# A decode kernel over two attention layers: one second-pass unit of four rows placed ahead of the next row's kept units

## The chip, the cores and the metric

The kernel runs on one core of one Trainium2 chip. The metric is the device time of one execution in microseconds (us). The time before is the median of five runs, 1151.18 us (1147.98, 1152.47, 1147.93, 1151.68 and 1151.18 us). Where this text says "the profile", it means one further look at the same kernel: an execution of 1147.98 us whose instructions and transfers were recorded.

## What is computed

Eight rows (a batch of 8, one token each, 448 numbers per row) go through attention, a small mixer and MLP, attention again with the same weights and the same cache, and the mixer and MLP again:

```python
def _A_ref(x, k_cache, v_cache, wq, wo):          # Hq = 16 heads, 8 KV heads, Sk = 4096, Dh = 256
    q = (x @ wq) as [B, 16, 1, 256]
    scores = einsum("bhqd,bhkd->bhqk", q, repeat(k_cache, 2)) * 256 ** -0.5
    o = einsum("bhqk,bhkd->bhqd", softmax(scores), repeat(v_cache, 2))
    return o as [B, 1, 4096] @ wo
...
x = x + _A_ref(_layernorm(x), K, V, wq, wo)
x = x + _B_ref(_layernorm(x), w1, w2, w3, w4)     # with one token the shifted parts are zero:
x = x + _A_ref(_layernorm(x), K, V, wq, wo)       # what is left is x1 + gelu(layernorm(x1) @ w3) @ w4
x = x + _B_ref(_layernorm(x), w1, w2, w3, w4)
```

K and V of one row are 8 x 4096 x 256 numbers of two bytes each, 33.6 MB for both. Both attention layers read all of them, and the query of the second reading of a row exists only when the first reading of that row, its output projection, its MLP and its second query projection are done.

## The kernel before, in words

**Units.** A unit is one pass over one pair of KV heads of one row. I write A for the first attention layer's pass and B for the second's: A3.1 is the first pass over row 3, pair 1, and B3.1 the second pass over the same data. A row has four pairs (0 to 3), so there are 64 units. Each is cut into four K chunks and four V chunks of 1 MB. The list `tasks` (L489 to L501) is the order of the units, written out by hand.

**Items.** `items` (L505 to L510) turns the units into single chunks: K chunk j is followed by the V chunk of four K chunks earlier (`LAG` = 4). The main loop (from L664) walks over the items. A K chunk is transposed on DVE in two instructions (L547), and PE multiplies it with the spread query (`scores`, L555). After four K chunks ACT takes the exponentials (L564) and PE transposes them (L577). A V chunk is multiplied on PE (`pv`, L596).

**Slots and loads.** All chunks live in 15 slots of 1 MB (`NC`, L61). `loads` (L516) is the items in order without those that need no load, and `emit_loads` (L522) issues the next load from SP whenever a slot has come free: always in the order of `loads`, so the list of units also sets the order of the transfers.

**Kept chunks.** Eleven chunks of a row stay in their slots from its first pass to its second: all eight of pair 3 and the first three K chunks of pair 2 (`kept`, L63). Pairs 2 and 3 are `keep`, pairs 0 and 1 are `free` in the code. From the last kept load of a row until the second pass of pair 3 gives slots back, only four slots are left to rotate.

**The chain.** Between the two passes of a row stands a sequence of small dependent steps: softmax sums, output projection (L318), norm, MLP (L336, L318), norm, query projection (L274). Its generator `chain` (L441) is added after the last first-pass unit of the row (L735) and is stepped from the main loop by `step` (L645), twice per item, so that its 30 counted steps are spread evenly up to the first item of the row's second pass. `last` (L462) does the smaller work that follows a finished second pass in the same way.

**The order around the change.** For rows 1 to 4 the order before is, with b the row whose second pass runs:

```
B(b).3  B(b).2  |  A(b+1).2  A(b+1).3  |  B(b).0  B(b).1  A(b+2).0  A(b+2).1  |  B(b+1).3  B(b+1).2 ...
```

The chain of row b+1 runs in the units between A(b+1).3 and B(b+1).3. At the two ends of the list (the chains of rows 0, 1, 6 and 7) three units stand there rather than four:

| chain of row | units between its two kept passes |
|---|---|
| 0 | A1.0 A1.1 A2.0 |
| 1 | B0.0 B0.1 A2.1 |
| 2, 3, 4, 5 | B(b).0 B(b).1 A(b+2).0 A(b+2).1, with b = 1 to 4 |
| 6 | B5.0 A7.0 A7.1 |
| 7 | B5.1 B6.0 B6.1 |

Of the kernel before, what the change touches and what calls it, by code (L numbers as in the profile page):

```python
# [17 lines left out]
def kernel(  # L18
# [28 lines left out]
    Bn, Sq, D = A_x.shape  # L47
# [438 lines left out]
    keep = sorted({gp for gp, _, _ in kept})  # L486
    free = [gp for gp in range(GP) if gp not in keep]
    assert Bn > 2 and free == [0, 1] and GP == 4
    tasks = [(0, 0, gp) for gp in free + keep] + [(0, 1, gp) for gp in free]  # L489
# [2 lines left out]
    tasks += [(0, 2, free[0])]  # L492
    for b in range(Bn):
        tasks += [(1, b, gp) for gp in keep[::-1]]
        if b + 1 < Bn:
            tasks += [(0, b + 1, gp) for gp in keep]
        if b == Bn - 2:
            tasks += [(1, Bn - 3, free[-1])]
        tasks += [(1, b, gp) for gp in (free[:-1] if b == Bn - 3 else free)]
        if b + 2 < Bn:  # L500
            tasks += [(0, b + 2, gp) for gp in (free[1:] if b == 0 else free)]  # L501


    nk = 4 * len(tasks)
# [159 lines left out]
    for idx, it in enumerate(items):  # L664
        n, kv, c = it
        ps, b, gp = tasks[n]
# [157 lines left out]
```

## Time and profile before

| what | value |
|---|---|
| median of five runs | 1151.18 us |
| profiled execution | 1147.98 us |
| its span, first to last instruction | 1146.2 us |
| PE (matmul) busy | 702.8 us, 61% |
| DVE busy | 548.1 us, 48% |
| ACT busy | 113.6 us, 10% |
| moved by the DMA engines | 457.52 MB, 399 GB/s over the span |
| chunk loads | 200 of K and 224 of V, 1024 KB each |

The span is the time between the first and the last recorded instruction; 1.8 us of the device time lie around it. A row of "windows" gives, for a stretch of the span in us, its length, the busy time of each engine with its number of instructions, the granted clock of TensorE as a share of full speed (PEclk), the busy share of the DMA engines, and the rate in GB/s at which they moved data. A chunk is 1.0486 MB.

### The profile page before, as it was taken

Reading aid. Unit: us, or ns where it says so; the run is one execution under the profiler, and the core shown is the slowest. Engines: PE = TensorE matmul, PEld = TensorE weight load, DVE = VectorE, ACT = ScalarE, POOL = GpSimd, SP = SyncE. Lnnn points to the kernel's source line nnn. Section 1 sums busy time; section 2 is a strip of 40 time slices with the busy share of each in tenths; the row PEclk is TensorE's granted clock in tenths of the full one; section 3 lists DMA queues with packets and bytes.
Section 4 is the critical chain, followed back from the end, with each engine's and each line's share of the span. In section 5 each row is a group of like instructions: output and inputs, shape, how many; then the busy total and the mean of one; then the engine's idle time right before and its main releaser. Section 6 shows DMA issues by size and latency. Waiting matters only on the chain.

```text
span 1146.2 us, 36707 instructions
## 1 busy us (share of the span) xinstructions
PE 702.8 (61%) x17177; PEld 512.9 (45%) x17177; DVE 548.1 (48%) x904; ACT 113.6 (10%) x234; POOL 15.6 (1%) x25
## 2 busy tenths in 40 slices
PE   3144677457755667556764667646765477547786
PEld 2023455345533445344542455425543365426566
DVE  5145453445444544445355553446434553546352
ACT  0001011100110011101110101010010101010100
POOL 0000000000000000000000000000000000000000
PEclk9999998655755556555565557555575557555655
DMA  9999999999999999999999999999999999999993
GB/s 353 376 420 419 407 367 411 419 416 379 406 420 414 387 388 420 420 404 397 398 419 420 407 406 410 420 421 391 398 420 420 414 384 418 418 419 394 414 420 134
DMA packets 68349, 457.52 MB, mean 399 GB/s; under 512 B 6999, under 2 KB 13030, under 8 KB 13542
## 3 DMA queue, kind: packets, MB, share of 16 engines
q1 hardware_dynamic: 68198, 455.19, 97.9%
q8 instruction: 134, 2.20, 0.8%
q14 instruction: 17, 0.14, 0.0%
HBM read 455.15 MB, written 0.01 MB: 397 GB/s over the span
## 4 chain that ended last, share of the span: by engine, by line
DMA 66%; PE 15%; DVE 12%; SPq 3%; issue 3%; POOL 1%; ACT 0%; POOLq 0%; DVEq 0%; ACTq 0%
DMA slot<-in_A_k_cache_dram 62%; DVE slot L547 10%; PE sc L555 5%; PE o L596 3%; DMA slot<-in_A_v_cache_dram 3%; SPq L148 2%; PE y_ps L318 2%; PE q_ps L274 1%; DMA wq_sb<-in_A_wq_dram 1%; SPq L539 1%; DVE qbd L300 1%; PE o L610 1%; PE o L318 1%; PE misc L381 0%; PE h_ps L336 0%
## 5 line engine op out<-in xcount | busy, mean ns | idle before, releaser
L547 DVE STREAM_TRANSPOSE slot<-slot 128x1024 uint32<-128x1024 uint32 x400 | 472.7, 1222 | 383.2 <-DMA slot<-in_A_k_cache_dram 375.0
L555 PE MATMUL sc<-slot,qbd 128*8 128x128 bf16 x8192 | 280.1, 286 | 344.7 <-DVE slot L547 290.7
L555 PEld LDWEIGHTS <-qbd 128*8 128x8 bf16 x8192 | 193.5, 105 | 429.8 <-issue 296.7
L596 PE MATMUL o<-slot,ptw 128*8 128x256 bf16 x3968 | 242.1, 387 | 54.0 <-DMA slot<-in_A_v_cache_dram 30.7
L564 ACT ACTIVATE p_n<-sc 128x512 bf16<-128x512 f32 x64 | 84.4, 1318 | 780.6 <-PE sc L555 780.6
L596 PEld LDWEIGHTS <-ptw 128*8 128x8 bf16 x3968 | 108.4, 109 | 91.6 <-issue 43.1
L318 PEld LDWEIGHTS <-wo_sb 128*128 128x128 bf16 (+1 forms) x1600 | 64.7, 124 | 16.5 <-issue 15.8
L318 PE MATMUL y_ps<-OT,wo_sb 128*128 128x1 bf16 (+1 forms) x1280 | 55.5, 177 | 3.0 <-issue 3.0
L384 DVE RECIPROCAL rz<-misc 128x8 f32<-128x8 f32 (+1 forms) x33 | 6.3, 192 | 94.8 <-PE misc L381 94.8
L274 PEld LDWEIGHTS <-wq_sb 128*128 128x128 bf16 x1152 | 34.0, 104 | 19.1 <-issue 17.4
L274 PE MATMUL q_ps<-xb,wq_sb 128*128 128x1 bf16 (+1 forms) x1152 | 35.6, 166 | 11.2 <-DMA wq_sb<-in_A_wq_dram 3.6
L584 ACT CAST ptw<-misc 128x128 bf16<-128x128 f32 x64 | 17.5, 273 | 207.5 <-PE misc L577 159.3
L411 PEld LDWEIGHTS misc<-R,o_sb 128*128 128x128 f32 x124 | 26.0, 293 | 11.3 <-issue 11.2
L318 PEld LDWEIGHTS <-w_sb 128*128 128x128 bf16 (+1 forms) x630 | 25.8, 125 | 7.3 <-issue 5.2
L411 PE MATMUL misc<-R,o_sb 128*128 128x8 f32 x124 | 28.9, 343 | 0.0
L232 POOL TENSOR_TENSOR t<-t,nhalf 128x2 f32<-128x2 f32 (+1 forms) x17 | 10.7, 630 | 1071.6 <-DVE t L239 973.0
L318 PE MATMUL y_ps<-HT_t,w_sb 128*128 128x1 bf16 (+1 forms) x560 | 24.2, 177 | 0.5 <-DVE HT_t L359 0.5
L300 DVE TENSOR_SCALAR qbd<-misc,quad 128x64 bf16<-128x64 f32 x64 | 13.8, 278 | 21.0 <-PE misc L294 21.0
L381 PE MATMUL misc<-zm,one 128*128 128x8 f32 (+1 forms) x66 | 17.9, 344 | 6.7 <-ACT ptw L584 6.7
L336 PEld LDWEIGHTS <-w_sb 128*128 128x128 bf16 x560 | 17.1, 104 | 9.5 <-issue 9.1
L336 PE MATMUL h_ps<-xb,w_sb 128*128 128x1 bf16 (+1 forms) x560 | 17.9, 166 | 4.9 <-DVE xb L249 4.6
L381 PEld LDWEIGHTS misc<-zm,one 128*128 128x128 f32 x66 | 15.0, 282 | 11.5 <-ACT ptw L584 8.4
(92 smaller groups left out, 208.0 us busy)
## 6 DMA issues: line engine op xcount, KB each, us to landing
slot<-in_A_v_cache_dram SPq DMA_DIRECT2D x224, 1024.0 KB, 12.3
slot<-in_A_k_cache_dram SPq DMA_DIRECT2D x200, 1024.0 KB, 15.7
wo_sb<-in_A_wo_dram SPq DMA_DIRECT2D x1, 3584.0 KB, 26.6
wq_sb<-in_A_wq_dram SPq DMA_DIRECT2D x3, 1024.0 KB, 6.9
w_sb<-in_B_w_dram SPq DMA_DIRECT2D x1, 1568.0 KB, 12.7
w_sb<-in_B_w_dram SPq DMA_DIRECT2D x3, 448.0 KB, 26.8
wq_sb<-in_A_wq_dram SPq DMA_DIRECT2D x2, 256.0 KB, 9.9
w_sb<-in_B_w_dram SPq DMA_DIRECT2D x2, 112.0 KB, 9.0
```

Source lines behind the costliest of these rows:

```text
L148: nc.sync.dma_start(t[:, fc * cols : (fc + 1) * cols], src[fc * 128 : fc * 128 + 128, :])
L274: nc.tensor.matmul(q_ps[:, j * Hq + h, :], w, xbs(nb)[:, xi, :], start=(fc == 0), stop=(fc == 3),)
L300: nc.vector.tensor_scalar_mul(qbd[:, :, :, a, :], qs.rearrange("p e (f g u h) -> p (e f) u g h", f=2, u=2, h=2)[:, :, u], quad[:, a : a + 1],)
L318: nc.tensor.matmul(r, w[:, i, lo:hi], rhs(i), start=(first and fc == 0 and i == rows[0]), stop=(stop and i == rows[-1]), skip_group_check= ...
L336: nc.tensor.matmul(h_ps[:, c * nb : c * nb + nb], w, xbs(nb)[:, xi, :], start=(fc == 0), stop=(fc == 3),)
L381: nc.tensor.matmul(z_ps, ones, zm[:], start=True, stop=True)
L411: nc.tensor.matmul(ot_ps[:, j], o_sb[:, 128 * j : 128 * j + 128], R[:], start=True, stop=True)
L547: nc.vector.transpose(w, w)
L555: nc.tensor.matmul(sc[32 * k : 32 * k + 8, 128 * x : 128 * x + 128], qbd[:, ep, gp].rearrange("p a h -> p (a h)"), kv[:, k, 2 * half + e2, ...
L564: nc.scalar.activation(p_sb[:].rearrange("p t i x -> p x t i"), sc[:].rearrange("p (x t i) -> p x t i", x=4, t=4), ACT.Exp, scale=scale_ex ...
L584: nc.scalar.copy(ptw[:, :, :, 6:8], pt_ps.rearrange("p t k (a h) -> p a (t k) h", a=4),)
L596: nc.tensor.matmul(o_ps[32 * q : 32 * q + 8, 256 * (g // 4) : 256 * (g // 4) + 256], ptw[:, a, 4 * (y % 4) + y // 4, w : w + 8], v[:, y * ...
```

## The change

For b = 1 to 4 the unit B(b).0 is taken from behind A(b+1).3 and put ahead of A(b+1).2:

```
before: B(b).3 B(b).2        A(b+1).2 A(b+1).3 B(b).0 B(b).1 A(b+2).0 A(b+2).1 B(b+1).3
after:  B(b).3 B(b).2 B(b).0 A(b+1).2 A(b+1).3        B(b).1 A(b+2).0 A(b+2).1 B(b+1).3
```

All other units stand where they stood. `items`, `loads` and the due times of the stepped generators are derived from the list and move with it.

```diff
     for b in range(Bn):
         tasks += [(1, b, gp) for gp in keep[::-1]]
-        if b + 1 < Bn:
+        if b == Bn - 2:
             tasks += [(0, b + 1, gp) for gp in keep]
-        if b == Bn - 2:
-            tasks += [(1, Bn - 3, free[-1])]
-        tasks += [(1, b, gp) for gp in (free[:-1] if b == Bn - 3 else free)]
-        if b + 2 < Bn:
-            tasks += [(0, b + 2, gp) for gp in (free[1:] if b == 0 else free)]
+            tasks += [(1, Bn - 3, free[-1])] + [(1, b, gp) for gp in free]
+        elif b == Bn - 1:
+            tasks += [(1, b, gp) for gp in free]
+        else:
+            early = 0 < b < Bn - 3
+            tasks += [(1, b, free[0])] * early + [(0, b + 1, gp) for gp in keep]
+            tasks += [(1, b, gp) for gp in free[early : 1 if b == Bn - 3 else 2]]
+            if b + 2 < Bn:
+                tasks += [(0, b + 2, gp) for gp in (free[1:] if b == 0 else free)]
```

## The prediction

> **What bounds the kernel now.** I read the page's slices and its chain of work first, then the rate of the transfers stage by stage. On the page:
>
> ```profile
> DMA  9999999999999999999999999999999999999993
> GB/s 353 376 420 419 407 367 411 419 416 379 406 420 414 387 388 420 420 404 397 398 419 420 407 406 410 420 421 391 398 420 420 414 384 418 418 419 394 414 420 134
> ...
> DMA 66%; PE 15%; DVE 12%; SPq 3%; issue 3%; POOL 1%; ACT 0%; POOLq 0%; DVEq 0%; ACTq 0%
> ```
>
> The DMA engines are busy in every slice but the last, and the chain of work runs through loads. But the rate in GB/s is not flat: it stands at 419 to 421 and dips once per row. So the time is bytes over rate, and what can be won is in the dips. 457.52 MB at 420 GB/s would take 1089.3 us; the span is 1146.2 us, so 56.9 us are lost. To place them I cut the span by units, at the ACT instruction (L564) that ends a unit's scores. The stretches from the end of B(b).3 to the end of A(b+1).3 lose nothing; one of them, lengthened by the first unit behind it:
>
> ```profile
> 297.00:361.00 64.00, 36.73 (x884) 25.36 (x887) 31.59 (x33) 6.97 (x14) 0.00 (x0) 0.59 1.01 420
> ```
>
> (The last column is 420, as in six more such stretches.) The stretches from the end of A(b+1).3 to the end of B(b+1).3, where the eleven chunks are kept, the chain of row b+1 runs and B(b+1).3 follows, hold the dips. For the chains of rows 0 to 7, in this order:
>
> ```profile
> core 0: us, PE busy (x) PEld busy (x) DVE busy (x) ACT busy (x) POOL busy (x), PEclk, DMA share, GB/s
> 105.40:181.10 75.70, 52.01 (x1274) 38.58 (x1266) 36.33 (x74) 6.98 (x15) 1.26 (x2) 1.00 0.99 391
> 224.00:297.00 73.00, 47.99 (x1150) 34.67 (x1140) 34.74 (x66) 7.03 (x16) 1.25 (x2) 0.51 1.00 396
> 340.50:434.60 94.10, 57.38 (x1362) 40.98 (x1362) 44.65 (x78) 8.75 (x19) 1.25 (x2) 0.52 1.00 399
> 478.60:571.30 92.70, 57.20 (x1362) 40.73 (x1355) 44.65 (x78) 8.75 (x19) 1.25 (x2) 0.52 0.99 401
> 615.80:706.30 90.50, 57.63 (x1362) 41.36 (x1362) 44.65 (x78) 8.69 (x18) 1.25 (x2) 0.51 1.01 408
> 751.30:843.10 91.80, 57.34 (x1362) 41.27 (x1355) 44.64 (x78) 8.69 (x18) 1.25 (x2) 0.51 1.01 405
> 888.00:959.00 71.00, 46.78 (x1160) 34.22 (x1152) 35.01 (x66) 6.79 (x14) 1.25 (x2) 0.51 1.00 402
> 1003.90:1075.00 71.10, 48.20 (x1150) 35.15 (x1139) 34.59 (x66) 7.07 (x16) 1.25 (x2) 0.51 1.00 407
> ```
>
> Lines 3 to 6 are the four-unit stretches that the change touches; the first two and the last two have three units already. The time lost in a stretch is its length times (1 - rate/420). That gives 5.23 and 4.17 us (rows 0, 1), then **4.71, 4.19, 2.59 and 3.28 us** (four units, sum 14.77, mean 3.69), then 3.04 and 2.20 us. (The remaining 27.5 us lie at the start and the end.)
>
> Where in a stretch? I cut two of them again: at the chain's first DVE step (L373) and at the copy of its last result (L283). A four-unit one, then the stretch of row 6 with three:
>
> ```profile
> 340.50:365.20 24.70, 10.18 (x228) 6.08 (x228) 11.78 (x10) 2.91 (x5) 0.00 (x0) 0.50 1.02 421
> 365.20:419.30 54.10, 36.70 (x854) 27.25 (x854) 29.05 (x58) 4.20 (x10) 1.25 (x2) 0.50 0.98 383
> 419.30:434.60 15.30, 10.50 (x280) 7.66 (x280) 3.83 (x12) 1.63 (x4) 0.00 (x0) 0.59 1.01 420
> ```
>
> ```profile
> 888.00:912.60 24.60, 10.27 (x244) 6.29 (x236) 12.59 (x15) 2.89 (x5) 0.00 (x0) 0.50 1.01 421
> 912.60:946.60 34.00, 27.64 (x660) 21.49 (x663) 18.93 (x45) 2.30 (x6) 1.25 (x2) 0.50 0.99 384
> 946.60:959.00 12.40, 8.86 (x261) 6.44 (x261) 3.50 (x8) 1.59 (x3) 0.00 (x0) 0.57 1.01 416
> ```
>
> The first part runs at 421 although slots are already few: loads issued earlier are still queued. The part with the chain runs at 383 and 384. After the chain the same four slots reach 420 and 416 (in two other stretches 385 and 373, 1.3 and 1.4 us lost, beside steps of `last`). So **the chain's steps cost, more than the four slots alone.** The queue shows why both are needed; loads and SP's longest waits from 361 to 425 us:
>
> ```profile
> slot<-in_A_v_cache_dram SPq DMA_DIRECT2D x14, 1024.0 KB, 8.6
> slot<-in_A_k_cache_dram SPq DMA_DIRECT2D x10, 1024.0 KB, 7.3
> ```
>
> ```profile
> SPq L539 <- DVE slot L547: 20.6, 8, 4.5
> SPq L539 <- PE o L596: 13.0, 10, 2.4
> ```
>
> A load lands there 7.3 to 8.6 us after its issue, about three chunks' worth at 2.50 us each (1.0486 MB at 420 GB/s), where a full queue, from 425 to 478.6 us, shows 19.8. SP sits waiting for transposes and PV products to free a slot. A step of the chain on PE or DVE that delays them by a few us empties a queue this short.
>
> **The change, part by part.** It removes and adds no instruction: the built order has 33962 entries on PE, 633 on DVE and 437 on SP in both versions, and the same bytes. It moves B(b).0 for b = 1 to 4: each time eight loads, eight transposes, 128 score and 64 PV matmuls, and one exponential. The loads pass, on SP's queue, the 16 loads of A(b+1).2 and A(b+1).3.
>
> Where it goes: between B(b).2 and A(b+1).2 all fifteen slots rotate and the rate is 420 (stretch 297 to 361, above). Eight loads more at that rate are 8 x 2.50 = 20.0 us of a full queue: the unit costs its bytes there and nothing else, its DVE work (8 x 1.22 = 9.8 us by the page) and PE work lying beside its transfers. If that cover were gone, the rate of the stretch would show it; its DVE is busy 31.6 of 64 us, so there is room. The kept loads come 20 us later, with the second pass that needs them equally later: nothing is late.
>
> Where it leaves: counted over the order of the items, from the chain's first item to the release of the first kept slot, 24 loads are issued before and 16 after. The unit's 20.0 us of bytes go; so does whatever was lost beside them. **The gain is therefore the loss per stretch with four units minus that with three, times four.** What the chain loses with it, it keeps: its instructions are the same, on 15 items rather than 23, so `step` takes its 30 counted steps at two per item instead of 1.3. What is queued behind a chain step on PE are scores and PV products, and behind those the loads: that is the one wait that grows denser.
>
> The trace of before does not show these rows with three units, so I bound them by the rows that have three. Lowest: 2.20 us (row 7), 4 x (3.69 - 2.20) = 6.0 us faster. Highest: 5.23 us (row 0), 4 x (3.69 - 5.23) = 6.2 us slower. Row 0 is the farthest: nothing but first passes, no `last` beside it, a clock of 1.00 against 0.51. I take the mean of the other three, (4.17 + 3.04 + 2.20)/3 = 3.14 us: 4 x (3.69 - 3.14) = **2.2 us faster**. The parts agree with that size: the chain's own stretch is 52.6 us long and loses 3.33 us on average with four units, 34.9 us and 2.49 with three (by the same cut: rates 383, 396, 402, 393 against 389, 384, 397, without row 0); the denser chain loses more per us (0.071 against 0.063) but for a shorter time.
>
> Sum against the profiled execution: 1147.98 - 2.2 = 1145.8 us. The median of the runs shown is 3.2 us above that execution, the runs lying in two groups near 1148 and 1152. I give the forecast on the median: 1151.18 - 2.2 = **1149.0 us**.
>
> Two places where the rows meet a rule. The trace holds 420 GB/s for 64 us on end and 383 in the worst chain stretch. The Trainium skill, "DMA: Bandwidth & Descriptors", Specifications, gives a limit of about 358 GB/s from HBM for a core; by it 383 would already be at the ceiling, nothing could be won, and the sum would be 0. The measurement decides: the ceiling here is 420. Second, PE is busy 36.7 of 54.1 us in the four-unit chain stretch and 27.6 of 34.0 in the three-unit one, the clock stands at 0.50 in both, and the stretch with 1.00 lost most. The skill's "TensorE: Matmul & The Clock Gate", Part 1, says that sustained work lifts the clock to full; an estimate by it would halve the denser chain's PE time and could take away all 14.77 us. The rows show no such lift at 81% busy, so I add nothing for it.
>
> **The rivals.** (1) *The slots are the cost, the chain only rides on it.* Then the loss goes with the loads issued in the narrow state, 16 instead of 24: 14.77/3 = 4.9 us faster, 1146.3 us. For it: the best three-unit rows, 3.04 and 2.20, are below the four-unit mean by 1.07, near the 1.23 that this asks. Against it: 420 GB/s after the chain with the same four slots.
>
> (2) *The loss belongs to the chain whole, whatever its length.* Rows 0 and 1 together with 6 and 7 have a mean of 3.66 us, the four-unit rows 3.69: 4 x 0.03 = 0.1 us, 1151.1 us. For it: both groups are centred on the same place in the span, and the losses fall with time whatever the number of units. Against it: row 0 carries the mean. This and my forecast are neighbours; both lie within 0.3% of the time before (3.45 us, about what a measurement of this kernel can tell from no change).
>
> (3) *The denser chain costs more than the unit saved: slower.* Two steps per item put two blocks of up to 64 small matmuls between a chunk's scores and the next PV product, in all four stretches. Price: as rows 0 and 1 in the mean, 4.70 us, 4 x 1.01 = 4.0 us slower, 1155.2 us. It decides above a loss of 3.69 + 3.45/4 = 4.55 us per stretch. For it: those two rows. Against it: rows 6 and 7, which have the same fifteen items at the same clock. A chain that is not done when B(b+1).3 starts would add to it; in the rows with three units its last copy is 12 us ahead of the end of B's scores, so it is done in time.
>
> That the change does not do what it says can be left out: the order of the instructions shows the moved unit and nothing else moved.
>
> **How the numbers follow.** Forecast (2.2 us faster, same): 0.36. Rival 1 (faster): 0.32. Rival 2 (same): 0.22. Rival 3 (slower): 0.10. So faster by over 0.3% 0.32, within 0.3% 0.58, slower 0.10. The range reaches down to the low bound of the unknown cost, 1151.18 - 6.0 = 1145.2 us, and up to row 1's loss in all four stretches, 4 x (4.17 - 3.69) = 1.9 us, 1153.1 us; the mean of rows 0 and 1 and row 0 itself are left outside.
>
> **What would show it.** Right: the four stretches from the end of A(b+1).3 to the end of B(b+1).3 are about 71 to 73 us long instead of 90.5 to 94.1, each loses 2.2 to 4.2 us against 420, and the stretch before each is 85 us at 420 instead of 65. Rival 1 shows losses near 2.5 in all four; rival 2 losses as before, 2.6 to 4.7; rival 3 losses over 4.55, with longer SP waits for scores and PV products. Wrong altogether: a rate under 420 in the stretch that takes the unit in, or a chain that ends after the first score of B(b+1).3.

## The result, and the profile after

The changed kernel takes 1151.32 us (median of 27 runs, 1147.31 to 1156.57); the kernel before takes 1150.96 us (median of 48 runs). The ratio is 1.0004, with a 95% interval of 0.9993 to 1.0015: **no difference**. The 2.2 us that were forecast are not there: 0.998 lies outside the interval. The profiled execution took 1153.14 us, its span is 1151.4 us. From its page, the slices and the chain of work:

```profile
DMA  9999999999999999999999999999999999999993
GB/s 354 376 419 420 409 378 401 419 409 367 409 420 420 394 392 420 420 421 380 389 420 420 421 379 396 420 420 404 386 406 420 409 376 416 420 416 371 411 420 147
...
DMA 69%; PE 14%; DVE 10%; SPq 3%; issue 3%; POOL 0%; ACT 0%; POOLq 0%; DVEq 0%; ACTq 0%
```

The bytes are the same and the dips are still there, one per row. The unit went where it was put, and at the price that was forecast. The stretch from the end of B1.3 to the end of A2.3 now holds B1.0; its columns are those of the windows above:

```profile
298.30:361.50 63.20, 35.17 (x884) 24.08 (x887) 31.47 (x33) 7.03 (x14) 0.00 (x0) 0.60 1.01 420
```

It is 63.2 us long at 420 GB/s; without B1.0 the same stretch of before (297.0 to 340.5 us) was 43.5 us: 19.7 us longer, for the 20.0 that were forecast. The eight stretches with a chain, for rows 0 to 7, all with three units now:

```profile
105.20:182.20 77.00, 52.73 (x1274) 39.06 (x1270) 36.43 (x75) 7.01 (x16) 1.26 (x2) 1.00 0.99 392
224.00:298.30 74.30, 48.60 (x1150) 34.88 (x1143) 34.74 (x66) 7.06 (x15) 1.25 (x2) 0.51 0.99 391
361.50:433.90 72.40, 47.80 (x1166) 35.26 (x1159) 35.27 (x70) 7.06 (x16) 1.25 (x2) 0.53 1.00 399
498.50:571.50 73.00, 48.84 (x1166) 35.83 (x1159) 35.40 (x70) 7.09 (x15) 1.25 (x2) 0.51 0.99 392
636.20:709.40 73.20, 48.31 (x1166) 35.70 (x1159) 35.32 (x70) 7.09 (x15) 1.25 (x2) 0.52 1.00 395
773.40:847.10 73.70, 48.94 (x1166) 36.03 (x1155) 35.46 (x70) 7.04 (x16) 1.25 (x2) 0.50 0.99 395
890.80:963.40 72.60, 47.31 (x1160) 34.59 (x1153) 35.02 (x66) 6.83 (x15) 1.25 (x2) 0.51 1.00 397
1007.60:1079.90 72.30, 48.37 (x1150) 35.30 (x1139) 34.69 (x66) 7.04 (x16) 1.25 (x2) 0.51 1.00 395
```

Lines 3 to 6 are some 73 us long instead of 90.5 to 94.1. But by length times (1 - rate/420) they lose 3.62, 4.87, 4.36 and 4.39 us, 17.2 in sum, where the four-unit ones lost 14.77. And the stretches of rows 6 and 7, whose units and order did not change, lose 3.98 and 4.30 us in this execution where they lost 3.04 and 2.20. In e3 below, which has the old order and in these two rows the same steps, they lose 3.62 and 3.76 (399 GB/s over 72.4 us, 398 over 71.7). So a row moves by one to two us between executions without any cause in its own code, and the 0.55 us per stretch that the forecast rested on is smaller than that. The sums 17.2 and 14.77 are those of one execution each, too: the profiled one of before lies 3.0 us below its kernel's median, this one 1.8 us above. The stretch of row 2, cut again at the chain's first and last step:

```profile
361.50:386.80 25.30, 10.18 (x244) 6.36 (x237) 12.53 (x14) 2.90 (x5) 0.00 (x0) 0.50 1.01 420
386.80:421.40 34.60, 28.22 (x662) 21.95 (x665) 19.32 (x49) 2.57 (x7) 1.25 (x2) 0.50 0.99 388
421.40:433.90 12.50, 9.41 (x264) 6.95 (x257) 3.43 (x9) 1.59 (x4) 0.00 (x0) 0.65 0.97 383
```

Queued loads carry the first part, as before. The chain's part lost 2.64 us and the part behind the chain 1.10, at 383 GB/s, where I had read 420 and 416 from two such lines. That part is no clean view of four slots in any of these lines. The kept K chunks of B(b+1).3 are scored in it and give their slots back: in the line of before at 420, PE begins on them at 427.50 us, and SP issues seven loads from 428.58 to 434.49 us, where it had issued four from 420.08 to 426.42. They are not transposed again either, so DVE is busy for only 3.83 of 15.3 us. PE is busy 28.22 of 34.60 us in the middle line, and the granted clock is still 0.50. SP's longest waits (us in total, times, longest) from 386 to 434 us:

```profile
SPq L543 <- PE o L600: 14.2, 9, 2.8
SPq L543 <- DVE slot L551: 10.2, 5, 3.4
```

It waits 14.2 us for PV products in 48 us, where the four-unit stretch of before had 13.0 us in 64: about the same total in a shorter time. For transposes it waits 10.2 us where it had 20.6, so the two waits together, 24.4 us in 48 and 33.6 in 64, are no denser than before.

### The profile page after: what moved, and what is told of

Its sections match the earlier page's. It is cut to its first block, busy times and chain, and to the rows that moved or that the text cites. A ratio compares the mean times of both kernels' runs of the same rounds, so it can differ in the third digit from the quotient of the medians.

```text
span 1151.4 us, 36703 instructions
## 1 busy us (share of the span) xinstructions
PE 703.6 (61%) x17177; PEld 514.1 (45%) x17177; DVE 548.7 (48%) x904; ACT 113.8 (10%) x234; POOL 15.6 (1%) x25
## 4 chain that ended last, share of the span: by engine, by line
DMA 69%; PE 14%; DVE 10%; SPq 3%; issue 3%; POOL 0%; ACT 0%; POOLq 0%; DVEq 0%; ACTq 0%
DMA slot<-in_A_k_cache_dram 64%; DVE slot L551 9%; DMA slot<-in_A_v_cache_dram 4%; PE sc L559 4%; PE y_ps L318 3%; PE o L600 3%; SPq L148 2%; PE q_ps L274 1%; DMA wq_sb<-in_A_wq_dram 1%; SPq L543 1%; PE o L614 1%; PE o L318 1%; PE h_ps L336 0%; DVE qbd L300 0%; POOL t L232 0%
## 5 line engine op out<-in xcount | busy, mean ns | idle before, releaser
L588 ACT CAST ptw<-misc 128x128 bf16<-128x128 f32 x64 | 17.5, 273 | 204.3 <-PE misc L581 155.2
L336 PEld LDWEIGHTS <-w_sb 128*128 128x128 bf16 x560 | 17.5, 104 | 13.9 <-issue 13.5
```

Source lines behind the costliest of these rows:

```text
L336: nc.tensor.matmul(h_ps[:, c * nb : c * nb + nb], w, xbs(nb)[:, xi, :], start=(fc == 0), stop=(fc == 3),)
L588: nc.scalar.copy(ptw[:, :, :, 6:8], pt_ps.rearrange("p t k (a h) -> p a (t k) h", a=4),)
```

## The experiments

Twelve kernels ran, each in five rounds beside the kernel before on the same chip. Ratios are to the kernel before, with the 95% interval.

| run | median us | ratio | interval |
|---|---|---|---|
| old order, no chain (e1) | 1139.31 | 0.9907 | 0.9879 to 0.9934 |
| changed order, no chain (e2) | 1137.93 | 0.9886 | 0.9861 to 0.9911 |
| old order, denser chain (e3) | 1155.28 | 1.0040 | 1.0018 to 1.0062 |
| changed order, one more narrow unit (e4) | 1154.49 | 1.0027 | 1.0009 to 1.0045 |
| changed, step behind PV (e5) | 1156.79 | 1.0045 | 1.0026 to 1.0063 |
| old, step behind PV (e6) | 1152.22 | 1.0006 | 0.9984 to 1.0028 |
| changed, all steps ahead of scores (e7) | 1162.16 | 1.0095 | 1.0064 to 1.0127 |
| changed, 10 kept (e8) | 1149.20 | 0.9980 | 0.9963 to 0.9998 |
| changed, step behind scores (e9) | 1168.34 | 1.0143 | 1.0116 to 1.0170 |
| old, 10 kept (e10) | 1148.55 | 0.9964 | 0.9949 to 0.9978 |
| changed, finer steps (e11) | 1164.25 | 1.0098 | 1.0071 to 1.0125 |
| changed, copy on ACT (e12) | 1152.30 | 1.0026 | 1.0007 to 1.0046 |

After the result I had two theories. Theory 1 was rival 2: the loss belongs to the chain whole. Theory 2: a narrow unit (one that runs with four rotating slots) has a price of its own and was saved, and the chain, which now runs its steps on 15 items rather than 23, took it back.

**The chain left out, in both orders (e1, e2).**

```diff
     def chain(b, st):
-        OT, y_ps = st["OT"], st["y"]
-        yield from half(st["o"], st["z"], 1, OT[:, :, :, 0])
...
         qT = chn.tile([128, NB2], BF16, tag="qT2", bufs=2)
-        yield from project_q(b, 1, qT[:].unsqueeze(2))
+        nc.vector.tensor_copy(qT[:], qT1[:, :, b])
         state[1, b] = {"qT": qT}
+        yield
```

(`first_half` is emptied likewise.)

> Left out: the whole chain between a row's two passes (softmax sums, output projection, MLP, second query projection); the second pass uses a copy of the first query. The order of the units is that of before (four units between the kept passes of rows 2 to 5). Theory 1, the chain's steps cause the loss and the narrow state of four slots costs next to nothing by itself: of the 29.4 us lost in the eight stretches of before, 25 or more go, 1122 to 1127 us. Theory 2, the narrow state costs about 1 us per unit and the denser chain of the change cost about as much, so that the two cancelled: some 10 us stay, 1130 to 1136 us. Under both the first-pass units keep their time.

> Left out: the same chain, in the changed order (three units between the kept passes). Theory 1: the same time as the old order without its chain, within 1.5 us. Theory 2: the four units taken out of the narrow state show now that no chain hides them, 4 us or so faster than the old order without its chain.

By the medians only 12.1 us went in the old order and 13.5 in the changed one. Theory 1 asked for 25 or more; theory 2, with 1130 to 1136 us, had the time too low as well. Over all eight stretches 23.1 us are still lost in e1 and 18.8 in e2, of 29.4 and 35.8 with the chain. The stretches of rows 2 to 5, old order and then changed order, both without a chain:

```profile
338.50:429.60 91.10, 43.42 (x1018) 28.13 (x1011) 40.08 (x45) 8.31 (x17) 0.00 (x0) 0.50 1.00 408
473.70:566.30 92.60, 43.31 (x1018) 28.02 (x1011) 40.18 (x45) 8.23 (x16) 0.00 (x0) 0.51 1.00 401
611.50:702.60 91.10, 43.56 (x1018) 28.13 (x1011) 40.18 (x45) 8.26 (x16) 0.00 (x0) 0.50 1.00 407
746.50:837.60 91.10, 42.16 (x1018) 27.47 (x1009) 40.08 (x45) 8.21 (x16) 0.00 (x0) 0.51 1.00 407
```

```profile
356.20:425.80 69.60, 34.11 (x822) 22.64 (x815) 30.59 (x37) 6.67 (x13) 0.00 (x0) 0.51 1.00 405
490.80:561.30 70.50, 34.65 (x822) 22.91 (x815) 30.59 (x37) 6.65 (x14) 0.00 (x0) 0.51 1.01 410
625.80:697.10 71.30, 34.11 (x822) 22.38 (x813) 30.70 (x37) 6.61 (x13) 0.00 (x0) 0.52 0.99 405
761.10:831.60 70.50, 34.41 (x822) 22.72 (x815) 30.60 (x37) 6.64 (x14) 0.00 (x0) 0.51 0.99 405
```

Without the chain these lines hold the units' own work and the few steps of `last`, and they still lose 2.60, 4.19, 2.82, 2.82 us (12.4) with four units and 2.49, 1.68, 2.55, 2.52 us (9.2) with three. So **the narrow state costs without the chain**. That a unit less of it costs less is likely from this pair and not shown by it: the difference is 3.2 us in these two executions, but row 1, the same in both, differs by 2.5 us (5.12 and 2.60); the ratios of the two runs differ by 0.0021, 2.4 us, with intervals that overlap. Theory 2 had 4. Theory 1 falls, and with it the sentence of the prediction that the chain costs more than the slots.

**The chain's density alone (e3).**

```diff
-    add_gen("chain", b, chain(b, st), idx + 1, first_of[(1, b), 0] - 1, 30)
+    add_gen("chain", b, chain(b, st), idx + 1, idx + 16, 30)
```

> Old order, but the chain of every row is due 15 items after its start, as in the changed order, rather than 23: four units between the kept passes, of which the last has no chain. Theory 1: no difference, 1151 us within 2 us, since the loss goes with the chain's steps and not with their distance. Theory 2: the price of the denser chain without the gain of the shorter narrow state, about 4 us slower than before, 1155 us.

1.0040 times before, 4.6 us slower (2.1 to 7.1), as theory 2 had it. The same units, slots and loads; the chain is done eight items earlier, 17.5 us in the stretch of row 2 (L283 at 401.8 us instead of 419.3). The four stretches:

```profile
341.00:435.70 94.70, 56.30 (x1362) 40.59 (x1351) 45.02 (x78) 8.62 (x18) 1.25 (x2) 0.52 0.99 393
481.00:573.50 92.50, 56.90 (x1362) 41.10 (x1351) 44.94 (x78) 8.64 (x18) 1.26 (x2) 0.51 1.00 397
617.90:711.00 93.10, 56.58 (x1362) 40.90 (x1354) 45.06 (x78) 8.67 (x19) 1.25 (x2) 0.51 1.00 402
755.50:849.10 93.60, 56.25 (x1362) 40.63 (x1351) 44.96 (x78) 8.66 (x19) 1.25 (x2) 0.52 1.00 396
```

They lose 6.09, 5.07, 3.99 and 5.35 us, 20.5 in sum. **About 1.1 us per stretch is the price of two steps per item instead of 1.3.** In units this kernel is also the changed one with its fourth narrow unit given back: from e3 to the changed kernel the ratio falls by 0.0036, 4.1 us, for four narrow units, and the two intervals do not overlap. One thing differs beside the unit. The steps of `last` start behind the chain in e3 (row 2: its first, L373, at 409.4 us) and beside it in the changed kernel (407.5 us, the chain's last at 421.4); what that costs, if anything, is in the 4.1 us and was not measured.

**One narrow unit more, without a chain in it (e4).**

```diff
-        tasks += [(1, b, gp) for gp in keep[::-1]]
+        tasks += [(1, b, free[0])] * (0 < b < Bn - 3) + [(1, b, gp) for gp in keep[::-1]]
...
-            tasks += [(1, b, free[0])] * early + [(0, b + 1, gp) for gp in keep]
+            tasks += [(0, b + 1, gp) for gp in keep]
...
-                elif done == 2:
+                elif done == 2 + (0 < b < Bn - 3) and ps == 1:
```

> Changed order, but for rows 1 to 4 the unit of pair 0 of the second pass comes ahead of the kept units instead of behind them: the chain has the same three units, and one more unit without a chain runs with four slots, in four stretches. Theory 1: the same time as the changed kernel, 1151 us within 2 us. Theory 2: four narrow units at about 1 us each, 1155 us.

1.0027 times before, 0.0023 or 2.6 us above the changed kernel; theory 2 had said 4, theory 1 none. Against before it is slower beyond its interval; against the changed kernel the two intervals touch. Its stretches with the unit, of rows 1 to 4:

```profile
223.30:316.50 93.20, 59.47 (x1360) 42.74 (x1355) 44.85 (x77) 8.96 (x20) 1.26 (x2) 0.50 1.00 404
359.00:453.10 94.10, 57.93 (x1368) 41.66 (x1361) 45.52 (x81) 8.95 (x19) 1.25 (x2) 0.52 1.00 397
497.50:590.20 92.70, 56.68 (x1368) 40.82 (x1357) 45.35 (x81) 8.97 (x19) 1.26 (x2) 0.54 1.00 401
634.40:730.20 95.80, 59.67 (x1376) 43.08 (x1372) 45.17 (x81) 8.99 (x20) 1.26 (x2) 0.50 1.00 400
```

Cut at the ends of the units, the added ones (B1.0 to B4.0, some 20.5 us each) lost 0.4, 0.9, 0.7 and 1.0 us. Whole stretches do not show it: those of rows 1 to 4 lose 17.5 us here and 18.0 in the changed kernel's profile, one execution each. So three ways give the price of a narrow unit by the ratios: 0.6 us (e1 to e2), 0.65 (changed to e4) and 1.0 (e3 to changed). They agree in sign, and the last is clear of its intervals.

**Where the denser chain's price comes from (e5 to e7, e9, e11, e12).** The two-and-two placement of the steps around a K and a V item was shifted. In e5 and e6 the step ahead of the PV products goes behind them:

```diff
-            step(idx)
+            if final:
+                step(idx)
...
         emit_loads()
         step(idx)
+        if kv == 1 and not final:
+            step(idx)
```

> Changed order; of the two chain steps of a V item, the one that stood ahead of the PV products now stands behind them, so that only one step, not two, lies on TensorE between a K chunk's scores and the next PV products. Theory 2a, the denser chain costs through the PV products that wait behind two steps in a row, which frees the V slots late: three to four us come back, 1147.5 us, and SP waits less for PV products. Theory 2b, the chain costs by its total work and its own waits between engines wherever its steps stand: 1151 us within 2 us.

> Old order with the same step moved behind the PV products. Theory 2a: rows 2 to 5 have 1.3 steps per item and seldom two in a row ahead of PV products, so little comes back there, and about one us in each of the four stretches that have three units: 1148 us, slower than or equal to the changed order with the same edit by 1 to 4 us, as the narrow units remain. Theory 2b: 1151 us within 2 us.

Theory 2a falls: the changed kernel got 4.7 us slower by it (1.0045 against 1.0004), and 2b, which had no change, falls too. The old order shows no loss by the same edit (1.0006). So where all eight stretches have two steps per item, the place of a step counts. That it is free with 1.3 is not shown to the microsecond: e6's interval goes up to 3.2 us, and the old order has two steps per item in the four stretches of rows 0, 1, 6 and 7 as well. In e7, which has that edit too, the step behind a K chunk's scores goes ahead of them as well:

```diff
             step(idx)
+            if not final:
+                step(idx)
             scores(sc_t[n % 2], slot, c, st["q"], gp)
```

> Changed order; all four chain steps of a K and a V item stand between the PV products and the next scores, none between scores and PV products. Theory 2a: V slots come free as early as without a chain, but four steps, up to some 4 us of TensorE, can stand ahead of the scores, whose transposes take 2.4 us: 1146 to 1149 us. Theory 2b: 1151 us within 2 us.

Slower again, 1.0095, outside what either theory had. e9 is the mirror image of e5: the step ahead of the scores goes behind them.

```diff
-            step(idx)
+            if final:
+                step(idx)
             scores(sc_t[n % 2], slot, c, st["q"], gp)
...
         emit_loads()
         step(idx)
+        if kv == 0 and not final:
+            step(idx)
```

> Changed order; the mirror image of the step moved behind the PV products: the chain step that stood ahead of a K chunk's scores now stands behind them, so three steps can lie between scores and the next PV products and one between those and the next scores. Theory 3a, what costs is the number of chain steps in a row between two products that free slots, so that the even placement of the changed kernel (two and two) is the best: as bad as the one-and-three placement, 1156 us. Theory 3b, the K chunk's way (transposes, then scores) is the tight one and each step ahead of the scores delays it: three to five us faster than the changed kernel, 1147 us.

1.0143, the slowest of all. Theory 3b falls; of 3a the direction holds (the even placement is the best that was tried), the size does not. Its four stretches lose 7.42, 7.15, 6.09 and 6.51 us:

```profile
366.80:442.80 76.00, 48.17 (x1170) 35.29 (x1164) 35.43 (x70) 7.19 (x16) 1.25 (x2) 0.52 0.98 379
506.70:583.70 77.00, 48.05 (x1174) 35.69 (x1170) 35.59 (x70) 7.15 (x15) 1.25 (x2) 0.52 0.98 381
647.20:722.40 75.20, 48.23 (x1170) 35.45 (x1162) 35.58 (x70) 7.08 (x15) 1.25 (x2) 0.52 0.99 386
785.80:861.80 76.00, 48.63 (x1166) 35.59 (x1157) 35.53 (x70) 7.12 (x15) 1.25 (x2) 0.51 0.98 384
```

Then the same work in smaller portions (e11), with a third `step` in the middle of `scores` and `pv`; the MLP's two projections are cut in the same way:

```diff
-                if h % 8 == 7:
+                if h % (4 if nb == 1 else 8) == (3 if nb == 1 else 7):
                     yield
...
-        yield from add_half(y_ps, OT, 1, 1, False, 2)
+        yield from add_half(y_ps, OT, 1, 1, False, 1)
...
-    add_gen("chain", b, chain(b, st), idx + 1, first_of[(1, b), 0] - 1, 30)
+    add_gen("chain", b, chain(b, st), idx + 1, first_of[(1, b), 0] - 1, 40)
...
         for y in range(16):
+            if y == 8:
+                between()
             q = y % 4
```

> Changed order; the same chain cut into steps of at most 16 matmuls (38 or so rather than 28) and taken at three places per item, the third in the middle of the scores and of the PV products, so that its work lies more evenly between the products. Theory 3a: the stretches lose some 4 to 8 us less, 1144 to 1148 us. If the chain's total work and its waits between engines cost whatever the cut: 1151 us within 2 us.

1.0098: slower, not faster, outside both expectations, so theory 3a in the form "steps in a row" fell too. The length of a step was not changed alone here: the third place lies inside the scores and PV products, and SP's waits for PV products from 386 to 434 us rise from 14.2 to 17.8 us, while those for transposes fall from 10.2 to 4.0. In the kernels with the denser chain DVE waits more for the chain's TensorE results, with the next transposes behind. Over the stretches of rows 2 to 5 I summed from the trace the idle time of DVE ahead of all its instructions but the transposes: 25.5 us before, 60.7 changed, 54.7 in e3, 71.0 in e5, 71.1 in e7, 78.9 in e11, 85.4 in e9, and in e6, which kept its time, 25.5 again. One such wait is that for the chain's last result (L283); idle us and times in the whole execution, before and then changed:

```profile
  PE q_ps L274: 18.5, 5
```

```profile
  PE q_ps L274: 28.6, 9
```

e12 takes just that wait off DVE:

```diff
-        nc.vector.tensor_copy(qT, q_ps[:])
+        if nb == 1:
+            nc.scalar.copy(qT, q_ps[:])
+        else:
+            nc.vector.tensor_copy(qT, q_ps[:])
```

> Changed order; the copy of the chain's last result (L283), ahead of which DVE stands 2.6 us in each of the four stretches with the next K chunk's transposes queued behind it, is done by ACT instead. Theory 4, the denser chain costs because DVE, taking its instructions in order, waits for the chain's TensorE results with transposes behind: of some 60 us of such DVE waits in the four stretches 10.6 go, and the kernel gets 2 to 4 us faster than the changed one, 1148 us. If these waits only accompany the loss: 1151 us within 1.5 us. If ACT's own queue (exponentials and the copies of the transposed weights) suffers by the wait: slower, 1153 us or more.

1.0026: not faster than the changed kernel; its interval takes in both no change and the third outcome, slower by ACT's queue. Of that no sign is in the trace: PE waits for ACT's copies of the transposed weights before its PV products 15.1 us in all, 14.3 in the changed kernel. The wait is gone from DVE (the sum is 51.4 us), the loss is not. So the DVE waits go along with the loss over these kernels, but **that they are its cause is not shown**, and for this one the run speaks against it. With five slots (e8, below) DVE waits 64.7 us by the same sum and the four stretches lose 6.0. What in the denser chain costs stays open; a kernel with the denser chain and several of its DVE waits removed was not run.

**A fifth slot (e8, e10).** Ten kept chunks instead of eleven, in both orders:

```diff
-    kept = [(GP - 1, kv, n) for n in range(4) for kv in range(2)] + [(GP - 2, 0, n) for n in range(3)]
+    kept = [(GP - 1, kv, n) for n in range(4) for kv in range(2)] + [(GP - 2, 0, n) for n in range(2)]
```

> Changed order with ten kept chunks per row instead of eleven, so five slots rotate in the narrow state and eight chunks more are loaded, 20.0 us at 420 GB/s. Theory 2, in both forms, puts the loss on a queue that four slots keep too short: if a fifth slot takes away half of the 36 us lost in the eight stretches of the changed kernel's profile, 1153 us; if it takes two thirds, 1147 us. If the loss were the chain's own time and not the slots, nothing would come back: 1171 us.

> Old order with ten kept chunks. With five slots the stretches of the changed order lost 11 us instead of 36. If both the narrow unit's price and the denser chain's price come from the short queue, both shrink to a third and the two orders stay equal: 1149 us within 2 us. If the chain's density acted by itself, the old order would be the faster one here, 1146 us.

Eight more chunks are loaded, and yet both kernels are faster than before. In the old order, 0.9964, rows 2 to 5:

```profile
339.70:429.20 89.50, 57.07 (x1362) 41.08 (x1355) 44.66 (x78) 8.76 (x19) 1.25 (x2) 0.51 1.01 415
476.80:566.30 89.50, 57.03 (x1362) 40.90 (x1355) 44.64 (x78) 8.79 (x19) 1.25 (x2) 0.51 1.01 413
613.90:703.50 89.60, 56.72 (x1362) 40.76 (x1354) 44.65 (x78) 8.74 (x19) 1.25 (x2) 0.52 1.01 414
750.90:840.00 89.10, 56.54 (x1362) 40.59 (x1355) 44.66 (x78) 8.74 (x19) 1.25 (x2) 0.52 1.00 412
```

In the changed order, 0.9980:

```profile
360.30:432.00 71.70, 48.22 (x1180) 35.76 (x1175) 35.39 (x70) 7.11 (x16) 1.25 (x2) 0.52 1.00 411
497.30:568.80 71.50, 47.97 (x1178) 35.63 (x1174) 35.37 (x70) 7.13 (x16) 1.26 (x2) 0.52 1.01 409
634.30:705.80 71.50, 47.83 (x1180) 35.53 (x1176) 35.36 (x70) 7.12 (x16) 1.25 (x2) 0.52 1.01 413
771.20:843.50 72.30, 47.65 (x1179) 35.50 (x1174) 35.42 (x70) 7.15 (x16) 1.25 (x2) 0.53 1.01 412
```

The old order loses 1.07, 1.49, 1.28 and 1.70 us, 5.5 in place of 14.77, the changed one 6.0 in place of 17.2. All eight stretches together lose some 10.5 us (old) and 11.5 (changed) in place of 29.4 and 35.8. So with a fifth slot about two thirds of the whole loss go, the narrow units' part and the chain's together; the loss needs the short queue. How much of each price is left was not run apart (a denser chain in the old order with ten kept). The two orders differ by 0.0016, within their intervals. e10 is the fastest complete kernel of the study; it beats both orders with eleven.

## Why the prediction was right, and where it was not

- **What bounds the kernel**: right. Bytes over 420 GB/s, and a loss only in the stretches with few slots. In the profiles of all twelve kernels with eleven kept chunks (before and changed among them) the span less the loss of the eight stretches, cut at the ends of the units, lies between 1113.8 and 1117.1 us, while the spans go from 1132.6 to 1171.4.
- **Where the unit goes**: right. 20 us at 420 GB/s, and nothing else late.
- **"The chain's steps cost, more than the four slots alone"**: wrong. It was read from two lines behind the chain, at 420 and 416. In that part kept slots are already coming back, so it does not show four slots; the same part of the changed kernel shows 383. Without any chain the four stretches lose 9 to 12 us.
- **The term 3.14 us, the mean of three native rows**: the step that failed. All three came from one execution, and the same rows measured 5.13, 3.98 and 4.30 us in the execution of the changed kernel. The four stretches lost 4.31 us on average rather than 3.14. The mean over rows in one trace looked like a sample of executions and was not one. The bound 2.20 to 5.23 us did hold.
- **The denser chain**: named ("the one wait that grows denser"), with 0.071 against 0.063 us lost per us, inside the term 3.14 and too small to matter. e3 gives it 1.1 us per stretch, as much as the unit saved.
- **The rivals**: rival 2 had the time, 1151.1 us, but its reason, a loss that knows only the chain, fell with e1 and e2. Rival 1's term is real (2.4 to 4.1 us for four units, where it had 4.9) and rival 3's is real (4.6 us, where it had 4.0 net). The change is the sum of the two, and they cancel: (-2.4 to -4.1) + 4.6, measured as +0.5 us (ratio 1.0004). The -4.1 is no check of that sum, since it is the changed kernel less e3; the two others leave +2, within the intervals.
- **The number**: 1149.0 us were forecast and 1151.3 measured, inside the range 1145.2 to 1153.1. That is in part luck: the forecast had one small gain of 2.2 us, and the runs show two terms of about twice that size and of opposite sign.
- **The clock**: right to add nothing for it. In the changed kernel PE is busy 28.22 of 34.60 us in the chain's part, its longest gap there is 0.91 us, and the clock stayed at 0.50, while the stretch of row 0 has 1.00 with 52.73 of 77.00 us busy. The Trainium skill, "TensorE: Matmul & The Clock Gate", Part 1, says that sustained work lifts the clock to full; this trace does not agree, if work at 82% with such gaps counts as sustained.

## What to carry to other kernels

Work that is spread over a window by due times has a price per density: when the window is shortened, the gain of the shorter window is to be set against the price of the denser work, and an experiment that changes the due time and leaves the window as it is separates the two. Where buffers held back for reuse leave too few for a running stream, count both sides in us: here one buffer more for the stream paid for eight loads more. And before a difference between rows of one trace is used as a term, look at how much the same rows differ between two executions.

## What was not expected

Where the small steps stand between a K chunk's scores and a V chunk's products was worth up to 16 us (1.0143 against 1.0004) in the changed order; in the old order only e5's edit was run, which cost 4.7 us in the changed one and showed nothing there (1.0006). And four slots in rotation, 1 MB each, did not hold 420 GB/s even with the chain left out: 400 to 410 GB/s over the stretches of rows 2 to 7 without a chain in the changed order, where five hold 409 to 413 in rows 2 to 5 with the chain.
